# Turning a 32-row memory block round: four identity products on TensorE, or VectorE's blockwise transpose and GpSimd copies

## The chip, the cores and the metric

The kernel runs on one core of a Trainium2 chip. The metric is device time in microseconds for one execution. TensorE multiplies matrices and writes to PSUM. VectorE (DVE), ScalarE (ACT) and GpSimd (POOL) work on tiles in SBUF, and VectorE and ScalarE also on PSUM. SyncE (SP) issues most transfers. Each engine works through its own queue in order and waits on semaphores for the others.

## The reference, cut to what matters

The input x (2048 tokens, width 1024) is normalised. The result is x plus a memory-augmented attention plus a token-mixing MLP. The attention goes in 64 segments of 32 tokens, each with 8 memory rows in front:

```python
for s in range(n_seg):
    h = jnp.concatenate([mem, xs], axis=1)          # 8 memory rows + 32 tokens
    q = jnp.einsum('btd,dhe->bhte', h, Wq)          # 32 heads of 128; k, v alike
    scores = jnp.einsum('bhqe,bhke->bhqk', q, k) * scale
    scores = jnp.where(mask[None, None], scores, -1000000000.0)
    p = _softmax(scores, axis=-1)
    o = jnp.einsum('bhqk,bhke->bhqe', p, v)
    o = jnp.einsum('bhte,hed->btd', o, Wo)
    mem = o[:, :M, :].copy()                        # memory of the next segment
    outs.append(o[:, M:, :])
```

## The kernel before, in words

The MLP comes first (to about 515 us of the profile), then the attention. For the memory of every segment after the first, the kernel uses an approximation that does not depend on the segment before, and checks it at the end (a slow path in a branch is there if the check fails; the profile does not show it taken). Only the first segment, whose memory is the input `mem0`, gets its 8 + 32 rows computed as they stand. It is called Z in the names below.

The attention runs through 32 steps: 4 blocks of 512 tokens (16 segments) times 8 groups of 4 heads. The order is written by hand in one loop. A step `s` has twelve chunks `c`:

- `c` 0 to 3: `q_chain`, queries (psQ, line 616; VectorE's addition into Q, line 623)
- `c` 4 to 7: `k_chain`, keys (psK, line 634)
- `c` 8 to 11: `v_chain`, values (psV, line 643)

In block 0 the memory's projections (psM, line 652) stand before the first and after the last chunk, giving QM and VM. Work of earlier steps is hung behind the chunks. `p` is the step before, `pp` the one before that:

- `c` 7: `scores(p)` (psS, line 667) and `values(pp)` (psO line 697, psE line 698, then VectorE's additions into oX, lines 702 and 709)
- `c` 7, or 11 where `p` is in block 0: `soft(p)`, the softmax of the 16 segments on VectorE (lines 673 to 682), with small pieces on GpSimd (lines 683 to 688)
- if `p` is in block 0: `first_scores(p)` at `c` 4, `first_soft(p)` at 8, `first_trans(p)` at 11
- if `pp` is in block 0: `first_values(pp)` at `c` 1

So the Z work occurs in eight steps. `first_scores` is all GpSimd: it gathers the first segment's queries, keys and values into QZ, KZ and VZ, with the 32 tokens ahead and the 8 memory rows behind. VM holds the memory's values with the head's 128 channels on the partitions; VZ needs them with the memory row on the partition. So 32 rows of VZ (32 to 63, of which 8 are data and the rest zero) come from a transpose of VM. Before the change this stands in `first_soft`: four products of VMZ with the identity on TensorE into the PSUM tile psVZ (line 737), and a ScalarE copy (line 738). Then come the scores psZ (line 741), their softmax into PZ (lines 743 to 750), PZ's transpose psZT (line 755), and in the next step psZO from VZ and PZT (line 762).

PSUM tiles named with `mm_tile` rotate through four buffers in the order in which they are asked for; psVZ is one of them. In head groups 5 to 7, `make_xm` (line 517) prepares the next block's input on VectorE behind chunks 2, 6 and 10. Weights come in 1 MB transfers by SyncE, each as a buffer comes free.

The tiles are made in `att_prep`, and GpSimd clears them once:

```python
            for nm in ("QZ", "PZ", "VMZ"):
                A[nm] = sm.tile([P, 4, P], BF16, name=nm)
                nc.gpsimd.memset(A[nm][:], 0.0)
```

Of the kernel before, what the change touches and what calls it, by code (L numbers as in the profile page):

```python
# [13 lines left out]
BF16 = mybir.dt.bfloat16  # L14
# [7 lines left out]
P = 128  # L22
# [9 lines left out]
M = 8  # L32
SEG = 32
NSEG = S // SEG
L = M + SEG
# [28 lines left out]
def kernel(  # L64
# [16 lines left out]
    nc = tc.nc  # L81
# [20 lines left out]
    def const_tile(name, arr, dt=BF16, later=False):  # L102
        a = _bf(arr) if dt == BF16 else np.asarray(arr, np.float32)
        d = nc.inline_tensor(a, name=name)
        t = cpool.tile(list(arr.shape), dt, name=name + "_sb")
        load = lambda: nc.gpsimd.dma_start(t[:], d.ap())
        if later:
            return load, t
        load()
        return t  # L110
# [10 lines left out]
    ident = const_tile("c_ident", np.eye(P, dtype=np.float32))  # L121
# [12 lines left out]
    def mm_tile(name):  # L134
        return psum.tile([P, 512], F32, tag="mm", bufs=4, name=name)
# [253 lines left out]
    with ExitStack() as p3:  # L389
# [95 lines left out]
        A = {}  # L485
# [11 lines left out]
        def need_w(nm, i):  # L497
            v, hg = A[nm, i]
            A[nm, i] = load_w(v, hg)

        def load_xT(b):
            A["x", b] = A["xvp"].tile([P, KT * 512], BF16, tag="x", bufs=2, name="xT", padded_shape=[P, KT * (512 + M)])
            nc.sync.dma_start_transpose(A["x", b][:].rearrange("p (k t) -> p k t", k=KT), xn_d[b * 512:(b + 1) * 512, :])

        def make_xm(b, ks=range(KT)):
            x3 = A["x", b][:].rearrange("p (k t) -> p k t", k=KT)
            if b == 0:
                A["m", 0] = A["xvp"].tile([P, KT, 512 + M], BF16, tag="x", bufs=2, name="xm")
                m3 = A["m", 0][:]
                nc.vector.tensor_copy(m3[:, :, 512:512 + M], MZ[:, :, 0:M])  # L510
                nc.vector.tensor_copy(m3[:, :, 0:SEG], x3[:, :, 0:SEG])
            else:
                m3 = A["m", b] = x3
            s0 = 1 if b == 0 else 0
            for k in ks:
                ms = MZ[:, k, 7 + 16 * b + s0:7 + 16 * b + 16]
                nc.vector.tensor_tensor(
                    m3[:, k, SEG * s0:512].rearrange("p (s i) -> p s i", i=SEG),
                    x3[:, k, SEG * s0:512].rearrange("p (s i) -> p s i", i=SEG),
                    ms.unsqueeze(2).to_broadcast((P, 16 - s0, SEG)), op=ALU.subtract)  # L520
# [10 lines left out]
        def att_prep():  # L531
            load_xT(0)
            for nm in "qkv":
                need_w(nm, 0)
            need_w("q", 1)
            make_xm(0)
            sm = A["sm"]
            A["EQ"] = sm.tile([P, 16, W], F32, name="EQ")
            nc.gpsimd.memset(A["EQ"][:, :, SEG:W], float(M))
            for nm in ("QZ", "PZ", "VMZ"):  # L540
                A[nm] = sm.tile([P, 4, P], BF16, name=nm)
                nc.gpsimd.memset(A[nm][:], 0.0)
            A["VZ"] = sm.tile([P, 512], BF16, name="VZ")
            nc.gpsimd.memset(A["VZ"][:], 0.0)
            A["SS"] = sm.tile([P, 16], F32, name="SSsum")
            nc.gpsimd.memset(A["SS"][:], 0.0)

        for tb in range(4):
            for f in range(FT):
                ps = mm_tile("ps3")  # L550
                w3 = w3a if f < FH else w3b
                for k in range(KT):
                    nc.tensor.matmul(ps[:], w3[:, k, (f % FH) * P:(f % FH + 1) * P], xn3Ts[tb][:, :, k, :], start=(k == 0), stop=(k == KT - 1))  # L553
                nc.scalar.activation(h3T[:, f, :], ps[:], ACTF.Gelu_apprx_tanh)  # L554
                filler(tb, 0, f)
                if f == 20:
                    load_R1(tb * 4)
            if tb == 0:
                load_chunk(0, 0)
            if tb == 3:  # L560
                rightx.close()
                att_open()
            for j in range(4):
                n = tb * 4 + j
                if j < 3:
                    load_R1(n + 1)
                R1 = R1s.pop(n)
                for ch in range(2):
                    ps = mm_tile("ps4")
                    for f in range(FT):  # L570
                        nc.tensor.matmul(ps[:], h3T[:, f, j * P:(j + 1) * P], w4t[f // 4][:, f % 4, ch * 512:(ch + 1) * 512], start=(f == 0), stop=(f == FT - 1))  # L571
                    nc.vector.tensor_tensor(R1[:, ch * 512:(ch + 1) * 512], ps[:], R1[:, ch * 512:(ch + 1) * 512], op=ALU.add)
                    filler(tb, 1, 2 * j + ch)
                nc.gpsimd.dma_start(R_v[:, n, :], R1[:])
                if tb == 3 and j == 0:
                    att_prep()
# [3 lines left out]
    wpool, xvp, qkv, smp = A["wpool"], A["xvp"], A["qkv"], A["sm"]  # L580
# [5 lines left out]
    VM = abig.tile([P, H, NZ], BF16)  # L586
# [3 lines left out]
    def hsl(hg):  # L590
        return slice(4 * hg, 4 * hg + 4)
# [8 lines left out]
    def new_step(i):  # L600
        s = Step()
        s.i = i
        s.b, s.hg = divmod(i, NHG)
        s.Q = qkv.tile([P, 4, 4 * TW], BF16, tag="Q", bufs=2, name="Q")
        if s.hg == 0:
            EMs[s.b] = smp.tile([P, NHG, 4, 4], BF16, tag="EM", bufs=2, name="EM")
            oTs[s.b] = smp.tile([P, H, 16], BF16, tag="oT", bufs=2, name="oT")
        s.xm = A["m", s.b]
        steps[i] = s
        return s  # L610
# [112 lines left out]
    QZ, PZ, VMZ, VZ = A["QZ"], A["PZ"], A["VMZ"], A["VZ"]  # L723

    def first_scores(s):
        s.KZ = smp.tile([P, 4, L], BF16, tag="KZ", name="KZ")
        nc.gpsimd.tensor_copy(QZ[:, :, 0:SEG], s.Q[:, :, 0:SEG])
        nc.gpsimd.tensor_copy(QZ[:, :, SEG:L], QM[:, hsl(s.hg), 0:M])
        nc.gpsimd.tensor_copy(s.KZ[:, :, 0:SEG], s.K[:, :, 0:SEG])
        nc.gpsimd.tensor_copy(s.KZ[:, :, SEG:L], s.K[:, :, 512:512 + M])  # L730
        nc.gpsimd.tensor_copy(VMZ[:, :, SEG:L], VM[:, hsl(s.hg), 0:M])
        nc.gpsimd.tensor_copy(VZ[0:SEG, :], s.V[0:SEG, 0, :])

    def first_soft(s):
        pv = mm_tile("psVZ")
        for hh in range(4):
            nc.tensor.matmul(pv[:, hh * P:(hh + 1) * P], VMZ[:, hh, :], ident[:], start=True, stop=True)
        nc.scalar.copy(VZ[SEG:2 * SEG, :], pv[SEG:2 * SEG, :])
        ps = mm_tile("psZ")[:, 0:4 * L].rearrange("p (h k) -> p h k", h=4)
        for hh in range(4):  # L740
            nc.tensor.matmul(ps[:, hh, :], QZ[:, hh, :], s.KZ[:, hh, :], start=True, stop=True)
        e = smp.tile([L, 4, L], F32, tag="eZ", name="eZ")
        nc.vector.scalar_tensor_tensor(e[:], ps[0:L, :, :], SCALE, mask40[0:L, :].unsqueeze(1).to_broadcast((L, 4, L)), op0=ALU.mult, op1=ALU.add)
        mx = smp.tile([L, 4], F32, tag="mxZ", name="mxZ")
        nc.vector.tensor_reduce(mx[:], e[:], axis=AX.X, op=ALU.max)
        nc.vector.tensor_tensor(e[:], e[:], mx[:].unsqueeze(2).to_broadcast((L, 4, L)), op=ALU.subtract)
        nc.scalar.activation(e[:], e[:], ACTF.Exp)
        nc.vector.tensor_reduce(mx[:], e[:], axis=AX.X, op=ALU.add)
        nc.vector.reciprocal(mx[:], mx[:])
        nc.vector.tensor_tensor(PZ[0:L, :, 0:L], e[:], mx[:].unsqueeze(2).to_broadcast((L, 4, L)), op=ALU.mult)  # L750
# [114 lines left out]
    for i in range(NS):  # L865
        s = new_step(i)
        p = steps.get(i - 1)
# [16 lines left out]
        if fz:  # L884
            at(4, first_scores, p)
            at(8, first_soft, p)
            at(11, first_trans, p)
# [80 lines left out]
    with tc.If(cond > 0):  # L968
        with ExitStack() as fctx:
# [17 lines left out]
            with tc.For_i(0, NSEG, 1) as i:  # L987
# [30 lines left out]
                for g8 in range(4):  # L1018
                    psS = fps.tile([L, 8, L], F32, tag="S", bufs=1)
                    nc.tensor.matmul(psS[:].rearrange("p h k -> p (h k)"), ident[:L, :L], mask40[:], start=True, stop=False, skip_group_check=True)  # L1020
                    for hh in range(8):
                        h = g8 * 8 + hh
# [3 lines left out]
                    sm = fr.tile([L, 8, L], F32, tag="sm")  # L1026
# [15 lines left out]
                    for hh in range(8):  # L1042
                        h = g8 * 8 + hh
# [50 lines left out]
```

## Time and profile before

| what | value |
|---|---|
| median of 5 runs | 1486.95 us (1485.71 to 1489.03) |
| the profiled execution's own time | 1487.75 us |
| its span, first to last instruction | 1486.0 us |
| TensorE clock granted | 1.0 throughout |
| the Z copies of `first_scores` on GpSimd, six a step | 0.21 to 0.60 us each |
| psVZ, products in all | 32, of 219 ns each from start to end |
| ScalarE's copy of psVZ | 8, of 576 ns |

The profile is of one execution. PE is TensorE's products, PEld its weight loads, which can run beside the products. Products are pipelined: one's time from start to end is longer than the distance between two starts. A row of a timeline gives start, length, engine, line, operation, tile written <- tiles read, shapes, the number of merged instructions, and in brackets how long the engine had been idle and what ended that. "issue" stands where the profile shows nothing that an engine waited for.

### The profile page before, as it was taken

Reading aid. Unit: us, or ns where it says so; the run is one execution under the profiler, and the core shown is the slowest. Engines: PE = TensorE matmul, PEld = TensorE weight load, DVE = VectorE, ACT = ScalarE, POOL = GpSimd, SP = SyncE. Lnnn points to the kernel's source line nnn. Section 1 sums busy time; section 2 is a strip of 40 time slices with the busy share of each in tenths; the row PEclk is TensorE's granted clock in tenths of the full one; section 3 lists DMA queues with packets and bytes.
Section 4 is the critical chain, followed back from the end, with each engine's and each line's share of the span. In section 5 each row is a group of like instructions: output and inputs, shape, how many; then the busy total and the mean of one; then the engine's idle time right before and its main releaser. Section 6 shows DMA issues by size and latency. Waiting matters only on the chain.

```text
span 1486.0 us, 28224 instructions
## 1 busy us (share of the span) xinstructions
PE 1469.4 (99%) x12314; PEld 759.9 (51%) x12432; DVE 500.7 (34%) x1017; ACT 352.0 (24%) x895; POOL 195.9 (13%) x450
## 2 busy tenths in 40 slices
PE   8999999999999999999999999999999999999998
PEld 7844444444444456666544444444444444444444
DVE  8184010010110213435341454541255432253443
ACT  5633202103113023333320222220122220032220
POOL 6142131211120200101000000000000000000000
PEclk9999999999999999999999999999999999999999
DMA  8599753454120745465531364541345442144301
GB/s 216 141 273 238 258 191 100 160 170 159 57 106 6 230 134 183 154 204 163 168 122 54 121 171 143 157 143 53 101 141 171 146 157 71 62 142 155 112 21 54
DMA packets 189184, 208.39 MB, mean 140 GB/s; under 512 B 50168, under 2 KB 157832, under 8 KB 189056
## 3 DMA queue, kind: packets, MB, share of 16 engines
q1 hardware_dynamic: 180768, 178.82, 40.2%
q0 software_dynamic: 8288, 27.72, 5.2%
q8 instruction: 99, 1.62, 0.5%
q14 instruction: 29, 0.24, 0.1%
HBM read 170.07 MB, written 25.17 MB: 131 GB/s over the span
## 4 chain that ended last, share of the span: by engine, by line
PE 97%; DVE 1%; DMA 1%; issue 1%; SPq 0%; ACT 0%; POOL 0%; ACTq 0%; POOLq 0%
PE psK L634 15%; PE psP L834 15%; PE psV L643 15%; PE psQ L616 15%; PE ps L553 13%; PE ps L571 13%; PE ps L366 4%; PE ps L265 2%; PE psS L667 1%; PE psO L697 1%; PE psM L652 1%; DVE st L204 1%; PE psvb L425 1%; PE psG L446 1%; DMA xn2T<-xn 0%
## 5 line engine op out<-in xcount | busy, mean ns | idle before, releaser
L834 PE MATMUL psP<-wo_sb,oX 128*128 128x512 bf16 (+1 forms) x1035 | 221.1, 372 | 1.1
L571 PE MATMUL ps<-w,hT_all 128*128 128x512 bf16 x874 | 193.7, 379 | 1.2
L634 PEld LDWEIGHTS <-w 128*128 128x128 bf16 x1280 | 125.1, 98 | 99.1
L616 PE MATMUL psQ<-xT,w 128*128 128x512 bf16 x744 | 169.1, 379 | 1.3
L643 PE MATMUL psV<-w,xT 128*128 128x512 bf16 x744 | 169.1, 379 | 1.3
L634 PE MATMUL psK<-xT,w 128*128 128x512 bf16 x763 | 169.4, 379 | 0.3
L834 PEld LDWEIGHTS <-oX 128*128 128x128 bf16 x1056 | 103.2, 98 | 117.1
L616 PEld LDWEIGHTS <-w 128*128 128x128 bf16 x1024 | 98.8, 98 | 115.9
L635 ACT CAST K<-psK 128x512 bf16<-128x512 f32 (+1 forms) x160 | 80.2, 501 | 303.9 <-PE psK L634 302.8
L644 ACT CAST V<-psV 128x512 bf16<-128x512 f32 x128 | 74.9, 585 | 289.9 <-PE psV L643 289.6
L623 DVE TENSOR_TENSOR Q<-psQ,QM 128x512 bf16<-128x512 f32 (+1 forms) x128 | 87.2, 685 | 167.1 <-PE psQ L616 106.5
L571 PEld LDWEIGHTS <-hT_all 128*128 128x128 bf16 x896 | 87.2, 98 | 103.8
L554 ACT ACTIVATE hT_all<-ps 128x512 bf16<-128x512 f32 x112 | 66.7, 597 | 283.5 <-PE ps L553 283.5
L643 PEld LDWEIGHTS <-xT 128*128 128x128 bf16 x768 | 74.1, 98 | 84.7
L553 PE MATMUL ps<-xn3T,w3a 128*128 128x512 bf16 x448 | 97.7, 379 | 0.0
L553 PE MATMUL ps<-xn3T,w3b 128*128 128x512 bf16 x448 | 97.7, 379 | 0.0
L702 DVE TENSOR_TENSOR oX<-psE,VM 128x128 bf16<-128x128 f32 x32 | 9.3, 292 | 217.5 <-PE psE L698 217.5
L709 DVE TENSOR_TENSOR oX<-psO,VM 128x96 bf16<-128x96 f32 (+2 forms) x256 | 82.0, 392 | 0.0
L840 DVE TENSOR_TENSOR ot<-psP,Rt 128x512 bf16<-128x512 f32 (+1 forms) x33 | 22.3, 675 | 167.6 <-PE psP L834 164.9
L553 PEld LDWEIGHTS <-w3b 128*128 128x128 bf16 x448 | 43.6, 98 | 51.9
L553 PEld LDWEIGHTS <-w3a 128*128 128x128 bf16 x448 | 43.5, 98 | 51.7
L481 DVE TENSOR_SCALAR xt<-xt,lnst 128x1024 bf16<-128x1024 bf16 x16 | 8.7, 545 | 179.5 <-POOL R L480 179.5
(162 smaller groups left out, 1254.3 us busy)
## 6 DMA issues: line engine op xcount, KB each, us to landing
w<-in_A_Wq_dram SPq DMA_DIRECT2D x32, 1024.0 KB, 5.4
w<-in_A_Wk_dram SPq DMA_DIRECT2D x32, 1024.0 KB, 5.4
w<-in_A_Wv_dram SPq DMA_DIRECT2D x32, 1024.0 KB, 6.5
R_scratch<-x POOLq DMA_DIRECT2D x16, 512.0 KB, 7.0
R<-R_scratch SPq DMA_DIRECT2D x16, 512.0 KB, 7.1
chunk<-in_A_Wv_dram SPq DMA_DIRECT2D x8, 1024.0 KB, 5.4
R_scratch<-R POOLq DMA_DIRECT2D x16, 512.0 KB, 4.1
chunk<-in_A_Wo_dram SPq DMA_DIRECT2D x8, 1024.0 KB, 6.5
```

Of the source, the lines that this page charges most:

```text
L366: nc.tensor.matmul(ps[:], hTB[:, k, o:o + P], w2_sb[:, k, ch * 512:(ch + 1) * 512], start=(k == 0), stop=(k == KT - 1))
L553: nc.tensor.matmul(ps[:], w3[:, k, (f % FH) * P:(f % FH + 1) * P], xn3Ts[tb][:, :, k, :], start=(k == 0), stop=(k == KT - 1))
L554: nc.scalar.activation(h3T[:, f, :], ps[:], ACTF.Gelu_apprx_tanh)
L571: nc.tensor.matmul(ps[:], h3T[:, f, j * P:(j + 1) * P], w4t[f // 4][:, f % 4, ch * 512:(ch + 1) * 512], start=(f == 0), stop=(f == FT - 1))
L616: nc.tensor.matmul(ps[:], w[:, k, hh * P:(hh + 1) * P], s.xm[:, k, 0:512], start=(k == 0), stop=(k == KT - 1))
L623: nc.vector.tensor_tensor(q3[:, j0:16, 0:SEG], p3_[:, j0:16, :], QM[:, 4 * s.hg + hh, z + j0:z + 16].unsqueeze(2).to_broadcast((P, 16 - j0 ...
L634: nc.tensor.matmul(ps[:, 0:c], w[:, k, hh * P:(hh + 1) * P], s.xm[:, k, h2 * c:(h2 + 1) * c], start=(k == 0), stop=(k == KT - 1))
L635: nc.scalar.copy(s.K[:, hh, h2 * c:(h2 + 1) * c], ps[:, 0:c])
L643: nc.tensor.matmul(ps[:], s.xm[:, k, m * P:(m + 1) * P], w[:, k, :], start=(k == 0), stop=(k == KT - 1))
L644: nc.scalar.copy(s.V[:, m, :], ps[:])
L709: nc.vector.tensor_tensor(oX[:, h0:h0 + hn, :].rearrange("p h (m c) -> p m h c", c=P)[:, m0:m1, :, SEG * j:SEG * (j + 1)], o4[:, 4 * m0:4 ...
L834: nc.tensor.matmul(ps[:, 0:w], oX[:, h, m * P:(m + 1) * P], wo_sb[:, h, cc], start=(h == 0), stop=(h == H - 1))
```

## The change

The four memory blocks of 128 channels x 32 columns in VMZ are transposed by VectorE, in `first_scores`. That instruction transposes each 32 x 32 block by itself and leaves it on its partitions, so head h's memory rows for channels 32q to 32q + 31 land on partitions 32q to 32q + 31 of a new tile VT. GpSimd then copies the four groups of partitions of VT into rows 32 to 63 of VZ, each into its 32 channels of every head. VMZ shrinks from 128 to 32 columns a head, with the memory in columns 0 to 7 instead of 32 to 39. The products with the identity, psVZ and ScalarE's copy are gone.

```diff
             for nm in ("QZ", "PZ", "VMZ"):
-                A[nm] = sm.tile([P, 4, P], BF16, name=nm)
+                A[nm] = sm.tile([P, 4, SEG if nm == "VMZ" else P], BF16, name=nm)
                 nc.gpsimd.memset(A[nm][:], 0.0)
...
         nc.gpsimd.tensor_copy(s.KZ[:, :, SEG:L], s.K[:, :, 512:512 + M])
-        nc.gpsimd.tensor_copy(VMZ[:, :, SEG:L], VM[:, hsl(s.hg), 0:M])
+        nc.gpsimd.tensor_copy(VMZ[:, :, 0:M], VM[:, hsl(s.hg), 0:M])
+        VT = smp.tile([P, 4, SEG], BF16, tag="VT", name="VT")
+        nc.vector.transpose(VT[:], VMZ[:])
         nc.gpsimd.tensor_copy(VZ[0:SEG, :], s.V[0:SEG, 0, :])
+        for q in range(4):
+            nc.gpsimd.tensor_copy(VZ[SEG:2 * SEG, :].rearrange("p (h q c) -> p h q c", h=4, q=4)[:, :, q, :], VT[SEG * q:SEG * (q + 1), :, :])
 
     def first_soft(s):
-        pv = mm_tile("psVZ")
-        for hh in range(4):
-            nc.tensor.matmul(pv[:, hh * P:(hh + 1) * P], VMZ[:, hh, :], ident[:], start=True, stop=True)
-        nc.scalar.copy(VZ[SEG:2 * SEG, :], pv[SEG:2 * SEG, :])
         ps = mm_tile("psZ")[:, 0:4 * L].rearrange("p (h k) -> p h k", h=4)
```

## The prediction

> **What bounds the kernel now.** I read the page's first parts, then the chain that ended last, then the timeline of PE round the edited place, then VectorE's and GpSimd's timelines there, and last the waits. The page comes first: who is full, and what the chain is made of.
>
> ```profile
> span 1486.0 us, 28224 instructions
> ...
> PE 1469.4 (99%) x12314; PEld 759.9 (51%) x12432; DVE 500.7 (34%) x1017; ACT 352.0 (24%) x895; POOL 195.9 (13%) x450
> ...
> q8 instruction: 99, 1.62, 0.5%
> ...
> PE 97%; DVE 1%; DMA 1%; issue 1%; SPq 0%; ACT 0%; POOL 0%; ACTq 0%; POOLq 0%
> ```
>
> PE (the matrix products) is busy for 99% of the span and makes 97% of the chain. VectorE (DVE) is busy for 34%, ScalarE (ACT) 24%, GpSimd (POOL) 13%. So PE time taken out counts nearly in full, and time added on DVE or POOL counts only if PE comes to wait for it. The line q8 is kept for later.
>
> Now PE's own timeline in step 2 of attention (columns: start, length, engine, line, tile):
>
> ```profile
> 591.95 0.62 PE L697 MATMUL psO<-PT,V 32*128 32x33 bf16 x60
> 592.50 0.23 PE L698 MATMUL psE<-BD,V 128*128 128x132 bf16 x1
> 592.57 1.89 PE L643 MATMUL psV<-w,xm 128*128 128x512 bf16 x7
> 594.30 0.39 PE L737 MATMUL psVZ<-c_ident_sb,VMZ 128*128 128x128 bf16 x4
> 594.52 0.26 PE L741 MATMUL psZ<-KZ,QZ 128*128 128x40 bf16 x4
> 594.62 5.34 PE L643 MATMUL psV<-w,xm 128*128 128x512 bf16 x24
> ```
>
> The lengths overlap, since products are pipelined; starts are what count. psVZ, which the change removes, holds PE from 594.30 to the start of psZ at 594.52: 0.22 us for four products. Then psZ takes 0.10. PE has no gap on either side, so nothing is being waited for here. It happens once in each of the eight steps in which the previous step belongs to block 0.
>
> **Removed from PE.** 8 places x 0.22 us = 1.8 us (0.22 again in step 3, from 620.75 to 620.97). Their weight loads lie beside the preceding product and add nothing of their own. psZ then follows a 512-wide product directly, as psZO does in block 0, and that group of four costs the same 0.10 us (580.60 to 580.70). So the saving is the full pitch.
>
> Here a rule of the Trainium skill gives another sum. The row is 0.22 us for four 128x128 transposes, 55 ns each in a stream that never stops. The page "VectorE: DVE Perf Modes", section "The three transpose paths", lists 390 ns for a TensorE transpose of 128x128 in bf16 and 311 ns for VectorE's blockwise one. By that figure the change would free 8 x 4 x 390 ns = 12.5 us, 0.8% of the kernel. I take the row: even a single psVZ product, start to end, is 219 ns in the tile's list, and most of that lies under its neighbours; the page prices an operation by itself. This choice decides the size of the forecast.
>
> **Removed from ACT.** The copy of psVZ into VZ, 8 x 576 ns = 4.6 us. ACT is idle for three quarters of the time, and the Exp of eZ behind it already waits for DVE (0.18 us in step 1, 0.78 in step 3). PZ, which that path makes, is written by 572.2 in step 1 and first read at 575.98. I cost the removal at nothing.
>
> **The PSUM ring.** psVZ took one of four rotating buffers, so later tiles move one place. psZ now reuses the buffer of psS's first half, and the next psV that of its second half. In step 1, where an activation table load delays the Exp, the second Exp ends at 569.53 and that psV would start at about 569.51: under 0.1 us, once. In later steps psO and psE lie between, and the Exp is long done.
>
> **Added on DVE and GpSimd.** These are their timelines, from step 1 into step 3, DVE first:
>
> ```profile
> 575.35 0.71 DVE L682 STREAM_TRANSPOSE PT<-Pn 128x512 bf16<-128x512 bf16 x1
> ...
> 584.56 0.66 DVE L623 TENSOR_TENSOR Q<-psQ,QM 128x480 bf16<-128x480 f32 x1 [1.07 <-ACT Q L622]
> 592.77 0.29 DVE L702 TENSOR_TENSOR oX<-psE,VM 128x128 bf16<-128x128 f32 x1 [7.55 <-PE psE L698]
> ```
> ```profile
> 578.46 0.29 POOL L729 COPY KZ<-K 128x128 bf16<-128x128 bf16 x1
> 578.70 0.21 POOL L730 COPY KZ<-K 128x32 bf16<-128x32 bf16 x1
> 578.85 0.21 POOL L731 COPY VMZ<-VM 128x32 bf16<-128x32 bf16 x1
> 580.92 0.60 POOL L732 COPY VZ<-V 32x512 bf16<-32x512 bf16 x1 [1.86 <-PE psZO L762]
> 592.79 0.26 POOL L683 CAST PT<-ET 128x16 bf16<-128x16 f32 x1 [11.27 <-PE psE L698]
> ...
> 605.80 0.60 POOL L732 COPY VZ<-V 32x512 bf16<-32x512 bf16 x1 [1.86 <-PE psZO L762]
> ```
>
> DVE gets one block transpose per step, 128 elements per partition. Its nearest row is L682, 0.71 us for 512 elements: at least a quarter of it, 0.18, at most all of it; I take 0.3. It stands behind the fourth Q addition, which ends at 585.22. VMZ has been ready since 579.06, so the new wait on GpSimd is empty, and what stands next in DVE's queue, L702, starts at 592.77 after 7.55 us idle. Cover: 7 us, for 0.3.
>
> GpSimd gets four copies of 32 partitions x 128 elements. The nearest row for the number of elements is L729, 0.29 us, with the next start 0.24 later. They move between groups of partitions, which no row shows; the upper bound I use is four times the 0.60 us of L732, 2.4 us. I take 4 x 0.24 = 1.0 us. They wait for DVE, which is new: GpSimd's queue now stands from 581.5 until 585.5 and finishes VZ at 586.6 (at 588 with the upper bound). Its next work, L683, starts at 592.79; cover at least 4.7 us. The reader of VZ is psZO of the next step, just before 605.80: some 18 us of cover. In the second block's first step, where the last of these lies, the fourth addition ends at 757.4, and psZO again comes in the step after. SP's queue and all transfers are untouched, and GpSimd issues no output transfers in these eight steps. The VMZ memset only shrinks.
>
> A rule that speaks against the change: three of the steps have this behind the fourth addition.
>
> ```profile
> 660.79 0.66 DVE L623 TENSOR_TENSOR Q<-psQ,QM 128x480 bf16<-128x480 f32 x1 [0.47 <-ACT Q L622]
> 661.37 0.68 DVE L517 TENSOR_TENSOR xT<-xT,MZ 128x512 bf16<-128x512 bf16 x1
> 669.00 0.29 DVE L702 TENSOR_TENSOR oX<-psE,VM 128x128 bf16<-128x128 f32 x1 [6.95 <-PE psE L698]
> ```
>
> L517 reads two tensors from SBUF, and would now run beside GpSimd's copies. By "SBUF — State Buffer", section "Who interferes with whom", such a VectorE instruction and a GpSimd instruction that reads SBUF exclude each other for the length of the one that came first. By the rule, L517 starts up to a copy (0.3 to 0.6 us) late and GpSimd loses up to 0.68 us, in three steps: 4 us at the very most, were it on the path. Before L702 there are 6.95 us, so either way the sum gets nothing. The trace has no such overlap to test it on.
>
> **The sum.** -1.8 us, +0 to 0.1 for the ring, nothing else on the path. The profiled execution took 1487.75 us for a span of 1486.0, 0.8 us above the median of the runs shown, so it stands for them: 1486.95 - 1.8 = 1485.2, which is -0.12%. About 0.2% (2.97 us) is what a measurement of this kernel tells from no change, so the likeliest outcome is real but too small to be told.
>
> **The rivals.** The waits of PE hold one more thing:
>
> ```profile
> PE psE L698 <- issue: 1.5, 1, 1.5
> ```
>
> In step 3, PE stands for 1.5 us ahead of psE with its weights loaded, waiting for nothing the profile shows. The line q8 of the page suggests a reason: 99 packets of instructions for 12,432 weight loads and as many products is about 250 PE instructions a packet (an estimate). psS, psO and psE are 125 pairs, 250 instructions, issued in 1.2 us (591.34 to 592.57 in step 2), where 125 products of 512 columns last 125 x 0.216 = 27 us. When a packet is used up this fast, its successor may be late. One of the 31 steps that have psO is hit. The change takes 8 instructions out of PE's stream in each of eight steps, so every packet border after the first moves against the work, by 8 up to 64 instructions. The stall can go, stay or come elsewhere.
>
> - The stall goes: -1.8 - 1.5 = -3.3, 1483.7 us, just faster than 0.2%. For: it hangs on a place in the stream, and that place moves by some 16 instructions by step 3. Against: another step may take it over. Chance 0.30.
> - Slower: the stalls multiply. Place: psE or the first psV after it. Price: 1.5 us each. Two more than now already turn the sign (+1.2); from four more it is past 0.2%: 4 x 1.5 - 1.8 = +4.2, 1491.2 us. For: in block 0 the K products are 260 wide and leave less time to fetch. Against: one in 31 is hit now. Chance 0.09.
> - Slower too: the chain GpSimd, DVE, GpSimd is late and psZO waits. It needs copies of over 4 us each; with 0.6 us of wait in each of eight steps, +4.8 - 1.8 = +3.0, 1490.0 us. Against: 18 us of cover. Chance 0.04.
> - That the change does not do what it says is excluded: PE's order loses exactly the four pairs of L737 in eight places and changes nowhere else.
>
> **How the numbers follow.** Main case 0.57, its own range 1484.0 to 1486.7 (a run-to-run scatter of 1485.7 to 1489.0 leaves about a microsecond on a median). With the vanished stall 0.30 (down to 1482.8) and part of the way to more stalls, the range is 1482.8 to 1488.3. Faster 0.30, same 0.57, slower 0.13.
>
> **What would show it.** Right: no L737 products; psZ starts 1.73 us after the first psV of its chunk; the transpose at 0.2 to 0.7 us behind the fourth addition; GpSimd's copies done before 588 in step 2; no new PE wait on DVE or POOL; PE busy down by about 2 us. Wrong: psZO or psE waiting for POOL, the copies at over 4 us, PE rows of "issue" at other steps, or a gap between psV chunks that psVZ had been filling.

## The result, and the profile after

The changed kernel takes 1484.82 us (median of 26 runs, 1483.56 to 1488.96), the kernel before 1487.47 us (46 runs). The ratio is 0.9981, 95% interval 0.9975 to 0.9986: 2.8 us less (2.1 to 3.7). That is the outcome called no change, to which the prediction gave 0.57, but only just: 0.2% is 3.0 us, inside the interval. It forecast 1485.2 us, which was 1.8 us below the kernel before.

The page of the profile after, cut to the lines that were shown of before:

```profile
span 1482.0 us, 28185 instructions
...
PE 1467.6 (99%) x12282; PEld 757.9 (51%) x12400; DVE 502.3 (34%) x1025; ACT 347.0 (23%) x887; POOL 206.4 (14%) x482
...
q8 instruction: 99, 1.62, 0.5%
...
PE 99%; issue 1%; DMA 0%; SPq 0%; DVE 0%
```

PE's busy time is down by 1.8 us, ACT's by 5.0; DVE has 1.6 us more and POOL 10.5. PE still makes the chain. PE's timeline in step 2, with start and length in the first two columns:

```profile
590.43 0.23 PE L698 MATMUL psE<-BD,V 128*128 128x132 bf16 x1
590.50 1.89 PE L643 MATMUL psV<-w,xm 128*128 128x512 bf16 x7
592.22 0.26 PE L741 MATMUL psZ<-KZ,QZ 128*128 128x40 bf16 x4
592.33 5.34 PE L643 MATMUL psV<-w,xm 128*128 128x512 bf16 x24
```

psZ now starts 1.72 us after the first psV, where it was 1.95 us; the group psZ still costs 0.1. The added work in the same step, DVE first:

```profile
582.49 0.66 DVE L623 TENSOR_TENSOR Q<-psQ,QM 128x480 bf16<-128x480 f32 x1 [1.06 <-ACT Q L622]
583.07 0.30 DVE L733 STREAM_TRANSPOSE VT<-VMZ 128x128 bf16<-128x128 bf16 x1
590.70 0.29 DVE L702 TENSOR_TENSOR oX<-psE,VM 128x128 bf16<-128x128 f32 x1 [7.33 <-PE psE L698]
```
```profile
583.43 1.28 POOL L736 COPY VZ<-VT 32x128 bf16<-32x128 bf16 x4 [3.98 <-DVE VT L733]
590.71 0.25 POOL L683 CAST PT<-ET 128x16 bf16<-128x16 f32 x1 [6.00 <-PE psE L698]
```

The transpose follows the fourth addition without a wait and takes 0.30 us. The copies end at 584.71, and GpSimd is then idle for 6 us. PE waits for none of it. What is new on PE is in the list of its waits (total in us, times, longest):

```profile
PE psO L697 <- issue: 0.6, 1, 0.6
PE psV L643 <- issue: 0.3, 1, 0.3
```

The one stall of 1.5 us in step 3 (a "stall" is here a wait of PE marked "issue") has become one of 0.3 us in step 3 and one of 0.6 us in step 5.

The two spans differ by 4.0 us, more than the medians do. Of that, 2.1 us is already there when psS of step 2 starts (591.34 before, 589.26 after), and only 0.2 of it can be the change, which begins in step 1. The rest is waiting in the MLP, which varies: PE's waits there for VectorE, ScalarE and a transfer add up to 4.3 us before and 2.7 us after, and two further kernels with the changed kernel's PE stream (e5 and e6 below) reach that psS at 589.92 and 591.04. The other 1.9 us arise from step 2 on.

### The profile page after: what moved, and what is told of

Read it like the earlier page. It is cut to its first block, busy times and chain, and to the rows that moved or that the text cites. A ratio compares the mean times of both kernels' runs of the same rounds, so it can differ in the third digit from the quotient of the medians.

```text
span 1482.0 us, 28185 instructions
## 1 busy us (share of the span) xinstructions
PE 1467.6 (99%) x12282; PEld 757.9 (51%) x12400; DVE 502.3 (34%) x1025; ACT 347.0 (23%) x887; POOL 206.4 (14%) x482
## 4 chain that ended last, share of the span: by engine, by line
PE 99%; issue 1%; DMA 0%; SPq 0%; DVE 0%
PE psK L634 15%; PE psP L834 15%; PE psV L643 15%; PE psQ L616 15%; PE ps L553 13%; PE ps L571 13%; PE ps L366 4%; PE ps L265 3%; PE psS L667 1%; PE psO L697 1%; PE psM L652 1%; PE psvb L425 1%; PE psG L446 1%; PE ps L294 0%; DMA x<-in_A_x_dram 0%
## 5 line engine op out<-in xcount | busy, mean ns | idle before, releaser
L643 PE MATMUL psV<-w,xT 128*128 128x512 bf16 x744 | 169.0, 379 | 1.3
L643 PEld LDWEIGHTS <-xT 128*128 128x128 bf16 x768 | 74.1, 98 | 84.7
```

The source lines that it names most:

```text
L643: nc.tensor.matmul(ps[:], s.xm[:, k, m * P:(m + 1) * P], w[:, k, :], start=(k == 0), stop=(k == KT - 1))
```

## The experiments

Theory A: the change takes 8 x 0.22 us off PE, the added work lies under cover, and the stalls hang on where an instruction stands in PE's stream, which the change shortens. Theory B: the stall before the change belongs to what the engines wait for in step 3, and became shorter because psVZ, its buffer and its copy left. Rival C: GpSimd's longer queue is on the path or near it.

**The stream made nearly as long as before (e1_pad).** In `first_soft` of the changed kernel:

```diff
-        ps = mm_tile("psZ")[:, 0:4 * L].rearrange("p (h k) -> p h k", h=4)
+        pz = mm_tile("psZ")
+        for _ in range(3 + s.i % 2):
+            nc.tensor.matmul(pz[:, 4 * L:4 * L + 1], ident[:], ident[:, 0:1], start=True, stop=True)
+        ps = pz[:, 0:4 * L].rearrange("p (h k) -> p h k", h=4)
```

> The changed kernel, with three or four one-column products of the identity (results unused) where psVZ stood, so that PE's stream is again nearly as long as before: at step 3 it is 2 instructions off the kernel before, where the changed kernel is 14 off. Theory A (the 1.5 us stall hangs on the place in PE's instruction stream): the stall of 1.4 to 1.6 us is back at psE or the first psV of step 3, and the 0.6 us one that the changed kernel has at psO of step 5 is gone (under 0.2 us left). Time: the small products cost about 0.1 us a step against 0.22, so 1.0 us below the kernel before, ratio 0.9993. Theory B (the stall belongs to what the engines wait for in step 3, and was shortened by taking psVZ, its buffer and its ScalarE copy out): stalls as in the changed kernel, 0.3 us in step 3 and 0.6 us in step 5, and the time 1.5 us below before.

Measured: 1485.96 us against 1487.35 for the kernel before, ratio 0.9989 (0.9983 to 0.9996). The stall is back in step 3, at the first psV, and step 5 has none:

```profile
615.97 0.23 PE L698 MATMUL psE<-BD,V 128*128 128x132 bf16 x1
617.75 2.60 PE L643 MATMUL psV<-w,xm 128*128 128x512 bf16 x7 [1.54 <-issue]
620.14 0.27 PE L741 MATMUL psZ<-c_ident_sb 128*128 128x1 bf16 x3
```

psVZ, its buffer and its ScalarE copy are still absent here, so B falls. The line also shows something else: seven psV take 2.60 us here, and 1.89 in step 2 above. The next two lines are windows of that place (length, PE busy and number, granted clock, DMA share, GB/s):

```profile
614.50:617.90 3.40, 1.86 (x130) 1.00 0.72 220
617.90:621.30 3.40, 3.35 (x17) 0.63 0.56 188
```

Behind the stall PE ran for a while at half clock; this profiled execution took 1487.43 us, 1.5 more than the median. The last section comes back to this.

**The whole stream moved, nothing else (e2_shift56 and e3_shift150).** Both are the kernel before with other warm-up products (the same columns in all, to 1%); the second has `87` and `70` for `40` and `154`:

```diff
-                nc.tensor.matmul(ps[:], fill[:, 0:P], fill[:], start=(i == 0), stop=(i == c - 1))
+                nc.tensor.matmul(ps[:, 0:154], fill[:, 0:P], fill[:, 0:154], start=(i == 0), stop=(i == c - 1))
...
-            warm(12)
+            warm(40)
```

> The kernel before, psVZ and all, with the 12 warm-up products of 512 columns at the very start written as 40 of 154 columns: the same columns, 56 PE instructions more ahead of everything. Theory A: step 3 loses its stall; step 6, which now lies as step 3 did to within some 10 instructions, gets one of 1.0 to 1.6 us; nothing else moves; time within 0.5 us of before (ratio 0.9997 to 1.0003). Theory B: the stall stays in step 3 with 1.5 us.

Measured: 1488.57 us against 1487.35, ratio 1.0003 (0.9995 to 1.0012). The list of PE's waits:

```profile
PE psO L697 <- issue: 1.8, 1, 1.8
PE psV L643 <- issue: 1.7, 1, 1.7
```

Step 3 has no stall, step 6 has one of 1.8 us (in psO). The other, 1.7 us in the second chunk of psV of step 4, was not foreseen. The profile is of the slowest of the 13 executions (1492.13 us), so the others need not have both stalls in full. Step 4 is the one in which the next block's input is loaded by a transposing transfer:

```profile
635.65 8.61 SPq L503 DMA_TRANSPOSE xT<-xn_scratch  x1
```

That transfer's issue ends at 644.26, some 2 us ahead of the stall. That it is what delays step 4 was not tried, by taking it away; the comparison of all stalls below has more for it.

> The kernel before with the warm-up as 87 products of 70 columns, 150 PE instructions more ahead of everything. Theory A: step 3 loses its stall, and steps 2 and 7 come to lie as step 3 did (5 and 2 instructions off): two stalls of about 1.5 us, and perhaps a small one (under 0.5) in step 4. Time 1.5 to 2 us over before, ratio 1.0010 to 1.0014. Theory B: one stall of 1.5 us in step 3, ratio 1.000.

Measured: 1489.48 us against 1487.35, ratio 1.0015 (1.0008 to 1.0022). Two stalls, in step 2 (first line) and in step 7 (second line), as forecast:

```profile
593.87 1.47 PE L643 MATMUL psV<-w,xm 128*128 128x512 bf16 x6 [1.23 <-issue]
...
719.67 0.17 PE L697 MATMUL psO<-PT,V 32*128 32x33 bf16 x1 [1.72 <-issue]
```

So without any change to the attention's work, a shift of PE's stream decides which steps stall, and here it moved the whole kernel by 2 us, not much less than the change under study did.

**The changed kernel moved by 68 (e4_after_shift68).** The edit of e2 in the changed kernel, with `46` products of `134` columns.

> The changed kernel with the warm-up as 46 products of 134 columns, 68 PE instructions more ahead of everything. Theory A: both stalls of the changed kernel (0.3 us in step 3, 0.6 us in step 5) go; step 6 comes to lie as step 3 of the changed kernel did and gets about 0.3 us. Time 0.6 us below the changed kernel: 3.0 to 3.4 us below before, ratio 0.9978 to 0.9980. Theory B: stalls and time as in the changed kernel, ratio 0.9981 to 0.9985.

Measured: 1484.59 us against 1487.35, ratio 0.9981 (0.9973 to 0.9990). The stalls of steps 3 and 5 went, and steps 4 and 6 have 0.3 us each (`PE psV L643 <- issue: 0.6, 2, 0.3`); the one in step 4 was not foreseen. The sum of the stalls fell from 0.9 to 0.6 us. The times cannot tell this kernel from the changed one, and nothing tried here is better.

**GpSimd's copies ten times over (e5_copies_x10).**

```diff
-        for q in range(4):
+        for q in 10 * list(range(4)):
```

> The changed kernel with the four GpSimd copies from VT to VZ made ten times over: 40 copies a step, about 10 us of GpSimd instead of 1. PE's stream is that of the changed kernel. Theory A (everything added lies under cover): GpSimd's next work, L683, starts late by some 3 us, no wait of PE on POOL appears, the stalls are those of the changed kernel (0.3 us in step 3, 0.6 in step 5), time as the changed kernel to 0.5 us. Rival C (GpSimd's queue is nearly on the path): psE or psZO waits for POOL, 1 us or more in each of seven steps, 5 us or more in all.

Measured: 1485.36 us against 1488.05 for the kernel before on the same chip, ratio 0.9982 (0.9974 to 0.9990), which is the changed kernel's. GpSimd's timeline in step 2:

```profile
584.09 14.12 POOL L736 COPY VZ<-VT 32x128 bf16<-32x128 bf16 x40 [3.98 <-DVE VT L733]
598.27 0.25 POOL L683 CAST PT<-ET 128x16 bf16<-128x16 f32 x1
```

L683 starts some 7 us late, more than the 3 expected (a copy took 0.35 us from start to start, not 0.24), and PE's waits are those of the changed kernel, 0.6 and 0.3 us. Rival C falls: ten times the copies cost nothing.

**Nothing added (e6_nothing_added).** The changed kernel without L733 and L736:

```diff
-        VT = smp.tile([P, 4, SEG], BF16, tag="VT", name="VT")
-        nc.vector.transpose(VT[:], VMZ[:])
...
-        for q in range(4):
-            nc.gpsimd.tensor_copy(VZ[SEG:2 * SEG, :]...[:, :, q, :], VT[SEG * q:SEG * (q + 1), :, :])
```

> The changed kernel without the VectorE transpose and without the four copies: the memory's rows of VZ stay zero, so the first segment's attention leaves out the memory's values. PE's stream is that of the changed kernel. It shows what the added work costs. Theory A: nothing, time as the changed kernel to 0.5 us (ratio 0.9979 to 0.9985 to before), stalls in steps 3 and 5 of the same size to 0.3 us. Rival C: faster than the changed kernel by 1 us or more.

Measured: 7188.56 us, so the total says nothing: without the memory's values the closing check sent the kernel through its slow path. The attention ahead of it can still be read. From step 4 to step 5 no kernel of these stalls, so the distance between their two psS is the cost of a step. The kernel before and the changed kernel, psS of steps 3 to 6, and this one, steps 4 and 5:

```profile
616.22 0.68 PE L667 MATMUL psS<-Q,K 128*32 128x33 bf16 x64
642.67 0.68 PE L667 MATMUL psS<-Q,K 128*32 128x33 bf16 x64
667.56 0.68 PE L667 MATMUL psS<-Q,K 128*32 128x33 bf16 x64
692.45 0.68 PE L667 MATMUL psS<-Q,K 128*32 128x33 bf16 x64
```
```profile
613.92 0.68 PE L667 MATMUL psS<-Q,K 128*32 128x33 bf16 x64
639.06 0.68 PE L667 MATMUL psS<-Q,K 128*32 128x33 bf16 x64
663.72 0.68 PE L667 MATMUL psS<-Q,K 128*32 128x33 bf16 x64
689.14 0.68 PE L667 MATMUL psS<-Q,K 128*32 128x33 bf16 x64
```
```profile
640.58 0.68 PE L667 MATMUL psS<-Q,K 128*32 128x33 bf16 x64
665.25 0.68 PE L667 MATMUL psS<-Q,K 128*32 128x33 bf16 x64
```

From step 4 to step 5 that is 24.89 us, 24.66 and 24.67. The change is worth 0.23 us a step, and what it adds costs nothing. Step 5's stall of 0.6 us is there too; step 3's 0.3 us is not in its list, though its PE stream is the changed kernel's, so the size of a stall also varies from execution to execution.

**psVZ three times over (e7_psVZ_x3).** In the kernel before, `for hh in range(4)` around the psVZ products became `for hh in 3 * list(range(4))`.

> The kernel before with the four products of psVZ made three times over, 16 PE instructions more at each of eight places. Theory A: the distance from psVZ to psZ grows from 0.22 to 0.66 us, so 8 x 0.44 = 3.5 us more; the stream's borders move too: step 3 lies now as step 5 of the changed kernel did (stall 0.6 to 0.8 us instead of 1.5), step 6 likewise gets 0.6 to 0.8. Sum 3.5 us over before, ratio 1.0022 to 1.0026. If a product cost the 390 ns of a transpose by itself, it would be 8 x 8 x 0.39 = 25 us.

Measured: 1493.34 us against 1488.05, ratio 1.0036 (1.0023 to 1.0049), 5.3 us more. Step 2:

```profile
593.37 0.83 PE L737 MATMUL psVZ<-c_ident_sb,VMZ 128*128 128x128 bf16 x12
594.04 0.26 PE L741 MATMUL psZ<-KZ,QZ 128*128 128x40 bf16 x4
```

Twelve products take 0.67 us, 56 ns each: the pitch of a stream, not a price of 390 ns. Steps 3 and 6 stall for 0.8 us each, as expected, and step 4 for 2.1 us, which was not. The added products are worth 8 x 0.45 = 3.6 us, and the stalls grew from 1.5 to 3.6 us, by 2.1: 5.7 us together, near the 5.3 measured.

**All stalls side by side.** The traces also hold every transfer of the queue of instructions, q8: packets of 16,384 bytes each. In the table, the weight load at which PE went on is counted among PE's recorded instructions (loads, a product for each, and waits that stand as instructions), and the last column is the time from the landing of the last packet ahead of it.

| kernel | step | us of stall | number of that load | us since the packet landed |
|---|---|---|---|---|
| before | 3 | 1.5 | 8899 | 1.4 |
| after | 3 | 0.3 | 8899 | 1.5 |
| after | 5 | 0.6 | 10179 | 1.3 |
| e1_pad | 3 | 1.5 | 8899 | 1.5 |
| e2_shift56 | 4 | 1.7 | 9666 | 1.4 |
| e2_shift56 | 6 | 1.8 | 10946 | 1.5 |
| e3_shift150 | 2 | 1.2 | 8386 | 1.5 |
| e3_shift150 | 7 | 1.7 | 11715 | 1.5 |
| e4_after_shift68 | 4 | 0.3 | 9666 | 1.4 |
| e4_after_shift68 | 6 | 0.3 | 10947 | 1.6 |
| e7_psVZ_x3 | 3 | 0.8 | 8899 | 1.4 |
| e7_psVZ_x3 | 4 | 2.1 | 9666 | 1.4 |
| e7_psVZ_x3 | 6 | 0.8 | 10946 | 1.6 |

e5 has the changed kernel's two stalls at the same numbers, e6 the one at 10179 alone. Every number is 194 or 195 above a multiple of 256 (8899 = 34 x 256 + 195), and the packet ahead of it is the one of that count, the 34th for 8899. The step and the tile change, the place in the stream does not. This is the border between two packets of 256 instructions, and what PE waits for is the next packet. Over 95 such borders in each of the nine traces, PE never passes one less than 1.2 us after its packet has landed. In the kernel before, PE passed the border ahead of step 3's psS at 615.69; the next packet started at 616.53 and landed at 617.56; by about 617.5 PE had used up the 256 instructions between, and it went on at 618.97.

For the stalls of step 4 the packet starts later, 3.9 to 4.0 us after the border before, where for the table's other stalls it starts 0.3 to 1.6 us after. In all nine traces the next packet behind the transposing transfer of step 4 starts 1.4 to 1.5 us after the end of its issue. That fits the account that this transfer holds the packet up, but it is not shown: delays of about 4 us occur at other borders too, with no such transfer.

## Why the prediction was right, point by point

- **psVZ's cost on PE, 8 x 0.22 = 1.8 us: right.** 0.23 us a step from psS to psS. The choice against the 390 ns of the page "VectorE: DVE Perf Modes", which would have made it 12.5 us, was the one that decided the size; e7 shows the pitch again with 56 ns. That the page prices an operation by itself was the prediction's reading: the section gives no condition for its figure.
- **ACT's copy worth nothing: right.** ACT lost 5.0 us, and no step without a stall became shorter by more than 0.24 us.
- **The PSUM ring, 0 to 0.1 us: right.** In step 1 psZ starts at 567.56 and the next psV at 567.66, 0.10 later, as in the other steps.
- **DVE 0.3 us, GpSimd 1.0 us under cover: right.** 0.30 and 1.28 us. The copies between groups of partitions, which no row had shown, take 287 ns, as much as the nearest row. e5 and e6 bound the cover from both sides.
- **The rule of "SBUF — State Buffer" against the change: it holds, off the path.** In the three steps with L517 behind the transpose, the four copies took 1.65 us instead of 1.28, and one copy 665 ns instead of 287; L517, which had started first, took 0.65 us and was not longer than before (0.68). PE saw nothing of it.
- **The stall: the mechanism was right, its size in the sum was not.** The main case left the stall as it was, and the first rival had it gone. What came lies between, with "issue" rows at another step, which the prediction had listed as a sign of being wrong. By the list of waits 1.5 us became 0.3 + 0.6. From psS to psS it is less: step 3 went from 26.45 to 25.14 us, 1.31 less, of which 0.22 is psVZ; step 5 went from 24.89 to 25.42 us, where psVZ alone would have made it 24.66. So the stalls are worth 1.09 - 0.76 = 0.33 us. The cause that the prediction suggested is borne out: e1 to e3 show that the place in the stream decides, and the landing of the packets shows what PE waits for. Its estimate of 250 instructions a packet is 256 in the table.
- **What the sum lacked.** 1.8 + 0.3 = 2.1 us, and the ratio says 2.8, with 2.1 at the edge of its interval. The rest has a candidate, the clock after a stall, in the last section.

The 1.8 us of the main case lies outside the measured 2.1 to 3.7. That the forecast of 1485.2 us comes within 0.4 us of the measured 1484.8 is in part luck: the kernel before measured 1487.47 us over 46 runs, where the forecast had started from 1486.95 over 5.

The rival of many stalls did not come with this change, but e3 and e7 show that it is real: two stalls for one cost 0.15% in e3. Its price of 1.5 us each is too low where the clock falls too: e1's step 3 took 28.06 us from psS to psS, and its step 2 took 24.76.

## What to carry to other kernels

Cost a small product in a full TensorE stream by the distance between starts, not by its length or by the price of a transpose by itself. Work moved off TensorE was free here because the other queues had slack at that place: even ten times the copies cost nothing. And before a difference of 0.1% is put down to an edit, look for "issue" stalls that moved. An edit that changes the number of TensorE instructions ahead of a dense stretch of small products can move, add or remove them by its place alone; here a warm-up in smaller pieces added 2 us (e3).

## What the runs showed of the hardware that was not expected

Behind a stall of 1.5 us TensorE's clock can be halved for a while. These are windows of e1, cut where its clock changes, and of the kernel before round its stall of the same size (columns as in e1 above):

```profile
615.36:618.77 3.41, 1.81 (x78) 1.00 0.76 231
618.77:622.18 3.41, 3.41 (x17) 0.50 0.28 90
```
```profile
616.39:619.80 3.41, 1.84 (x128) 1.00 0.68 222
619.80:623.22 3.42, 3.42 (x24) 1.00 0.40 132
```

In e1, PE was busy for 1.81 of the 3.41 us that hold the stall, and for the next 3.41 us its clock was one half. That costs 1.7 us. e2 has the same behind step 6 (0.50 over 697.54 to 700.95). The kernel before has no such drop in its profile, with PE busy for 1.84 us, and of the seven stalls of 1.2 us or more in the table only these two have it. What decides is open: e2's stall in step 4 and e3's in step 7 left PE no busier (1.70 and 1.65 us), without a drop. The page "TensorE: Matmul & The Clock Gate", section "What's actually happening", has a window of 3413 ns, and says that the clock falls after at least one idle window. The length agrees, but here PE was busy for about half of the window ahead of the drop.

The kernel before seems to have the drop in some executions. In the runs of these experiments, 17 of its 74 executions have a mean granted clock of 0.998, with a median of 1489.2 us; the 34 with 1.000 have 1487.1. Of the changed kernel's 28, one has 0.998 (1488.96 us). These are least counts, since the mean is a blunt sign: the profiled executions of e1 and e2 have 0.999 with the drop, and so has the changed kernel's without it, whose clock falls only behind PE's last product. If each such event costs 1.7 us, 17 in 74 against 1 in 28 makes 0.33 us on the mean, an estimate. Executions with 1.000 on both sides can be compared on the same chip: e5 is then 1.9 us faster than the kernel before (7 and 6 executions), where all its executions gave 2.7, and e4 2.4 us (9 and 28), where all gave 2.8. That is near the 2.1 us of the sum, so the clock can make up the rest; with so few executions, and none with the clock held fixed, this is not shown.
